# Turning C with VectorE and transfers in a fused state-space and feed-forward kernel

## The chip, the cores and the metric

The kernel runs on one core of a Trainium2 chip. The metric is the time of one execution on the device in microseconds. The core has a matrix engine (TensorE), a vector engine (VectorE), a scalar engine (ScalarE), a general engine (GpSimd, called POOL in the profile), and a synchronising engine (SyncE, SP) that here only issues transfers. All transfers run on the core's 16 DMA engines, whichever engine issues them. Results of TensorE go to PSUM, which has eight banks of 128 partitions by 512 f32 values; everything else lies in SBUF.

## The reference

```python
def A(x):                                   # x: (1, 2048, 448)
    Lam = Lambda_re + 1j * Lambda_im        # 448 complex modes
    dt = exp(log_dt)
    Lam_bar = exp(dt * Lam)
    B_bar = ((Lam_bar - 1) / Lam)[:, None] * (B_re + 1j * B_im)
    Bu = einsum("bld,pd->blp", x, B_bar)
    h[t] = Lam_bar * h[t-1] + Bu[t]         # over 2048 tokens
    return 2 * einsum("blp,dp->bld", h, C_re + 1j * C_im).real + x * Dskip
def B(x):
    return silu(x @ w1) @ w2                # 448 -> 1792 -> 448
g = sigmoid((x * gate_w).sum(-1))
out = g * A(x) + (1 - g) * B(x)
```

All inputs and the output are bf16. The kernel takes the state's rotation apart: with `Lam_bar = r * exp(i*phi)`, the input of each chunk is turned back by cos and sin of `phi * t`, a real scan with factor r runs over the tokens, and the states are turned forward again. The factor of B_bar is put into C instead, so that the readout weights are C times a complex number per mode.

## The kernel before

**Tiles.** The 2048 tokens are four chunks of 512 (`tc`) or sixteen blocks of 128 (`tb`). The 448 real and 448 imaginary parts of the modes lie in seven slots of 128 rows: slots 0 to 2 real, 4 to 6 imaginary, slot 3 the last 64 of both. For each chunk:

- `x_transposes` turns x on TensorE through PSUM into `xT` (line 508; the first chunk line 478), ScalarE or VectorE evicts it.
- `x_products` (line 663) makes tiles F (x times a 128-column block of w1; 14 a chunk) and B (x times a slot of B; 7 a chunk), two tiles as a pair in two PSUM banks. `evict` takes F through Silu on ScalarE into `aT` (line 634), and B into `U` (`UG`): for the first chunk on VectorE (line 640), else on ScalarE (line 642). Slot 3's halves are exchanged into slot 7 by two POOL transfers.
- `lanes(tc)` is the state-space part on VectorE: products of U with the tables COS and SIN (line 704 is the helper that records them all), seven scans into the f32 buffer `Gf` (line 736), a copy of Gf to bf16 in U by POOL transfers that convert (called Gb; the last chunk by ScalarE, line 746), and four products or sums that give the states `H`. For the first chunk the part ahead of the scans is written in pieces by block `b`, 512 or 1024 values a row; for the others over the whole chunk.
- `ffn2(tb)`, called G in the order: `aT` times w2 (line 774), evicted by ScalarE with the factor 1 - g into `fe` (line 780), which a POOL transfer adds onto `Tb` (line 782). `Tb` is xnat's memory, holding x * Dskip * g from `gates` (lines 836 to 850).
- `readout(tb)`, called C in the order: H times the readout weights `CP` (line 795), seven matmuls a block; VectorE multiplies by g and adds Tb (line 798), SP stores (line 801).

**Turning C.** C's rows are the output columns, and the readout wants the modes on the partitions. C is loaded into the memory of H2 after w2's load. `readout_weights(k)` (called `cp`) turns it in 64-row pieces on TensorE through two PSUM banks (line 814); ScalarE evicts one part times sc2 into `ct` (lines 822, 825), VectorE takes the other part from PSUM times sc1, adds ct and writes `CP` (lines 827, 830).

**Buffers.** U has two buffers, H four (the third shares its memory with C's rows, the fourth first holds B's rows).

**What sets the order.** The program makes a list of operations, each with the buffers that it reads and writes, a cost and a priority. A planner (`Plan.order`, lines 104 to 201) runs it through a model with those costs. TensorE's operations keep the order in which the program wrote them; every other engine takes, among the operations that could start earliest, the one with the lowest priority number. The result is one fixed list per engine, with waits on semaphores, and each engine goes through its list in order. Loads are numbered as they are written, and SP issues them in that order; POOL has a queue of its own for its transfers. The order of TensorE's work around the change is written out on lines 867 to 883.

Of the kernel before, what the change touches and what calls it, by code (L numbers as in the profile page):

```python
# [7 lines left out]
ALU = mybir.AluOpType  # L8
# [16 lines left out]
NFILL = 2  # L25
XCOL = [0, 128, 256, 320]
# [27 lines left out]
class Plan:  # L54
# [5 lines left out]
    RATE = {"pool": 300e3, "hw": 300e3}  # L60
    LAP = {"dve": 0.08, "act": 0.09}
# [42 lines left out]
    def order(self):  # L104
# [39 lines left out]
        while len(done) < len(ops):  # L144
# [5 lines left out]
            for eng, lst in cands.items():  # L150
# [9 lines left out]
                o = min((c for c in cand if c[0] <= t0 + 1e-9), key=lambda c: (c[1].prio, c[1].i))[1]  # L160
# [116 lines left out]
def bass_gated_mix__ssm_conv_s5__dense_activation_silu__prompt_kernel(nc, A_x, A_Lambda_re, A_Lambda_im, A_B_re, A_B_im, A_C_re, A_C_im,  # L277
               A_log_dt, A_Dskip, B_x, B_w1, B_w2, gate_w, out):
    with ExitStack() as ctx:
# [9 lines left out]
        xT = sb("xT", [128, 4, S_TOK], BF16)  # L289
# [3 lines left out]
        CP = sb("CP", [128, NSLOT, D_MOD], BF16)  # L293
        aT = [sb(f"aT{k}", [128, NFB, CH], BF16) for k in range(2)]
        UG = [sb(f"UG{k}", [128, 8, CH], BF16) for k in range(2)]
# [3 lines left out]
        H2C = sb("H2C", [128, 3840], BF16)  # L299
        H = [H2C[:, 0:3584].rearrange("p (s n) -> p s n", s=NSLOT) if k == 2 else sb(f"H{k}", [128, NSLOT, CH], BF16) for k in range(4)]  # L300
        Cnat = H2C[:, :].rearrange("p (b l) -> p b l", b=4)
        cnn = [f"H2_{s}" for s in range(7)] + ["H2_3i"]
# [91 lines left out]
        def load_w1(q, k, a, b):  # L394

            cols = slice(w1cuts[k], w1cuts[k + 1])
            src = B_w1[320:448, cols] if a == 3 else B_w1[128 * a:128 * b, cols].rearrange("(b p) f -> p b f", p=128)
            load(q, w1s[:, 3, cols] if a == 3 else w1s[:, a:b, cols], src, " ".join(f"w1_{k}_{i}" for i in range(a, b)),
                 256 * (b - a) * (cols.stop - cols.start))
# [11 lines left out]
        Bnat = H[3][:, :, 0:D_MOD]  # L411
        load("sp", Bnat[:, 0:3, :], A_B_re[0:384, :].rearrange("(b p) d -> p b d", p=128), "H3_0 H3_1 H3_2", 384 * 896)
        load("sp", Bnat[0:64, 3, :], A_B_re[384:448, :], "H3_3", 64 * 896)
        load("sp", Bnat[64:128, 3, :], A_B_im[384:448, :], "H3_3i", 64 * 896)
        load("sp", Bnat[:, 4:7, :], A_B_im[0:384, :].rearrange("(b p) d -> p b d", p=128), "H3_4 H3_5 H3_6", 384 * 896)
        btn = {s: [f"BT{s}_{h}" for h in range(2)] for s in range(7)}
        load_w1("sp", len(w1cuts) - 2, 0, 3)
        load_w1("sp", len(w1cuts) - 2, 3, 4)
# [8 lines left out]
        def load_C():  # L427

            for h in range(2):
                rows = lambda a: a[224 * h:224 * h + 224, :].rearrange("(b p) l -> p b l", p=56)  # L430
                to = Cnat[64 * h:64 * h + 56]
                load("sp", to[:, :, 0:448], rows(A_C_re), f"Cn0{h} " + (" ".join(cnn) if h == 0 else ""), 224 * 896)
                load("sp", to[:, :, 576:960], rows(A_C_im[:, 0:384]), f"Cn1{h}", 224 * 768)
                load("sp", to[:, :, 448:512], rows(A_C_im[:, 384:448]), f"Cn2{h}", 224 * 300)
                load("sp", to[:, :, 512:576], rows(A_C_re[:, 384:448]), f"Cn3{h}", 224 * 300)

        load_xn(1)
        load("sp", w2s[:, :, :], B_w2.rearrange("(fb p) d -> p fb d", p=128), "w2", F_FF * 896)
        load_C()
# [28 lines left out]
        def x0_transposes(q0, part, who):  # L468
# [12 lines left out]
            for h in range(2):  # L481
                src = lambda h=h: bk(tk, h).bitcast(BF16)[:, 0:256].rearrange("p (q b n) -> p q b n", q=2, n=64)
                dst = xT[:, q0:q0 + 2, 256 * part:256 * part + 256].rearrange("p q (b h n) -> p q b h n", h=2, n=64)[:, :, :, h, :]
# [11 lines left out]
        xn_of = {tc: {q: [f"xT{tc}_{h}" for h in range(2)] for q in range(4)} for tc in range(1, NCH)}  # L495
        xn_of[0] = {q: [f"xT0_{q}{part}{h}" for part in range(2) for h in range(2)] for q in range(4)}

        def x_transposes(tc, who):
# [13 lines left out]
            for h in range(2):  # L512
                src = lambda h=h: bk(tk, h).bitcast(BF16).rearrange("p (q b n) -> p q b n", q=4, b=4)
                dst = xT[:, :, tc * CH:(tc + 1) * CH].rearrange("p q (b h n) -> p q b h n", h=2, n=64)[:, :, :, h, :]
                if who[h] == "d":
                    DVE(lambda e, src=src, dst=dst: e.tensor_copy(dst, src()), [tk], [f"xT{tc}_{h}"], 0.69, 2.2, "xTe")
                else:
                    ACT(lambda e, src=src, dst=dst: e.activation(dst, src(), AF.Copy), [tk], [f"xT{tc}_{h}"], act_cost(1024), 2.2, "xTe")

# [73 lines left out]
        def b_transposes(s0, s1, who):  # L593
# [12 lines left out]
            PE(mm, [f"H3_{s}" for s in range(s0, s1)] + ["H3_3i"] * (s0 <= 3 < s1) + ["ident"], [tk], n * 4 * 0.0285, "BT")  # L606
# [16 lines left out]
        def evict(pair, tk):  # L623

            kinds = [t[0] for t in pair]
            for k, n in ((0, 2),) if pair[0][:2] == pair[-1][:2] and len(pair) == 2 else ((0, 1), (1, 1))[:len(pair)]:
# [10 lines left out]
                U, un = UG[tc % 2], f"U{tc % 2}_"  # L637
                dst = U[:, sl, :]
                if tc == 0:
                    DVE(lambda e, src=src, dst=dst: e.tensor_copy(dst, src()), [tk], [f"{un}{m}" for m in names], 0.15 + 0.53 * n, 2.6, "U")  # L640
                else:
                    ACT(lambda e, src=src, dst=dst: e.activation(dst, src(), AF.Copy), [tk], [f"{un}{m}" for m in names], act_cost(512 * n), 5, "U")  # L642
# [4 lines left out]
        def x_products(tiles, fill={}, wait=()):  # L647
# [10 lines left out]
            def steps(k, h, a, z):  # L658
                def body(pe):
                    for n, cut in list(enumerate(part[h]))[a:z]:  # L660
                        for b, ((i, p0), tile) in enumerate(zip(cut, pairs[k])):
                            tc = tile[1]
                            r = pe.matmul(bk(toks[k], b), weights(tile, p0, p0 + 64, i), xT[p0:p0 + 64, i, tc * CH:(tc + 1) * CH],  # L663
# [42 lines left out]
        def lanes(tc):  # L706
            pr = 20 + tc
            A, an = H[tc], f"H{tc}"
            U, u = UG[tc % 2], f"U{tc % 2}_"
            Gb = U  # L710
            t = f"L{tc}"
            if tc == 0:
# [20 lines left out]
            for s in (3, 0, 4, 1, 5, 2, 6) if tc else (0, 4, 1, 5, 2, 6, 3):  # L733
# [138 lines left out]
        for f in cp(0) + G(0, 1) + cp(1, 2) + G(2, 3) + cp(3):  # L872
            f()
# [45 lines left out]
```

## Time and profile before

| | |
|---|---|
| time, median of 3 runs | 141.66 us (141.62 to 142.56) |
| the profiled execution | 141.25 us |
| its span, first to last instruction | 139.5 us |
| mean granted TensorE clock | 0.998 of full |
| TensorE busy | 135.9 us (97%) |
| VectorE busy | 122.0 us (87%) |
| ScalarE busy | 90.3 us (65%) |
| GpSimd busy | 39.2 us (28%) |
| moved by the DMA engines | 14.71 MB, 17956 packets, 2835 of them under 512 bytes |

The profile is of one execution. Its time outside the kernel, 141.25, is 1.75 us more than the span, for what lies before the first and after the last instruction. A line of the groups names the code line, the engine, the operation, and the written and read tiles. In a timeline each row gives the start, the length, and how many instructions were merged into it; a bracket at the end gives the idle time before it and what ended it. VectorE's and ScalarE's operations overlap their neighbours by some 0.07 to 0.1 us, so an operation of 0.66 us can stand 0.57 to 0.59 us from the next.

### The profile page before, as it was taken

The numbers are of one execution on the slowest core, as the hardware profiler recorded it, in microseconds if no ns is written. First come the engines' busy times: TensorE is split into PE (matmuls) and PEld (weight loads), VectorE is DVE, ScalarE is ACT, GpSimd is POOL, SyncE is SP. The second block draws the span as 40 slices with busy tenths as digits, with TensorE's granted clock in tenths as the row PEclk, the third lists the DMA queues.
The fourth block names the chain that finished last, engine by engine and source line by source line (L and its number), as shares of the span: only waits on it lengthen the run. The fifth ranks groups of instructions, "written<-read, shape, count | busy, mean of one in ns | idle before, by whom it ended". The sixth has DMA issues, their size and how long they took to land.

```text
span 139.5 us, 3000 instructions
## 1 busy us (share of the span) xinstructions
PE 135.9 (97%) x1201; PEld 67.0 (48%) x1201; DVE 122.0 (87%) x179; ACT 90.3 (65%) x157; POOL 39.2 (28%) x72
## 2 busy tenths in 40 slices
PE   7999999999999999999999999999999999999992
PEld 2445454455544544455544544444455555555561
DVE  0319999999999999999999999999999999997053
ACT  3349768999989999823694887799931268312300
POOL 7134040100248440227733001824000314022220
PEclk9999999999999999999999999999999999999999
DMA  4998999510156770104976200674202322323242
GB/s 136 337 294 243 363 320 238 177 42 0 31 79 94 129 110 1 38 15 73 157 131 155 38 5 0 95 133 79 38 4 97 66 33 36 83 83 61 40 94 71
DMA packets 17956, 14.71 MB, mean 105 GB/s; under 512 B 2835, under 2 KB 17814, under 8 KB 17942
## 3 DMA queue, kind: packets, MB, share of 16 engines
q0 software_dynamic: 6064, 5.51, 24.8%
q1 hardware_dynamic: 11318, 8.65, 20.7%
q10 hardware_dynamic: 560, 0.36, 0.8%
q8 instruction: 9, 0.15, 0.4%
q14 instruction: 5, 0.04, 0.1%
HBM read 7.17 MB, written 1.84 MB: 65 GB/s over the span
## 4 chain that ended last, share of the span: by engine, by line
PE 97%; DVE 0%; issue 0%
PE ps L663 46%; PE ps L774 31%; PE ps L795 15%; PE ps L463 2%; PE ps L508 1%; PE ps L478 1%; PE ps L814 1%; PE ps L604 1%; DVE ot L798 0%; PE ps L675 0%; PE ps L464 0%; PE ps L536 0%
## 5 line engine op out<-in xcount | busy, mean ns | idle before, releaser
L663 PE MATMUL ps<-xT,w1s 64*128 64x512 bf16 x392 | 48.5, 378 | 0.0
L774 PE MATMUL ps<-w2s,aT 128*128 128x448 bf16 x224 | 43.2, 353 | 0.0
L634 ACT ACTIVATE aT<-ps 128x1024 bf16<-128x1024 f32 (+1 forms) x30 | 28.7, 969 | 8.5 <-PE ps L663 8.4
L774 PEld LDWEIGHTS ps<-w2s,aT 128*128 128x128 bf16 x224 | 21.7, 98 | 20.4 <-ACT xnat L849 0.4
L663 PEld LDWEIGHTS ps<-xT,w1s 64*128 64x128 bf16 x392 | 19.7, 94 | 22.3 <-DVE xT L486 0.7
L663 PE MATMUL ps<-xT,BT 64*128 64x512 bf16 x196 | 25.8, 376 | 0.0
L782 POOL DMA_DIRECT2D xnat<-fe x16 | 14.1, 900 | 37.9 <-ACT fe L780 37.2
L780 ACT ACTIVATE fe<-ps,g 128x448 bf16<-128x448 f32 x16 | 10.1, 632 | 21.1 <-PE ps L774 21.0
L390 POOL DMA_DIRECT2D UG<-Gf x27 | 14.7, 549 | 20.9 <-DVE Gf L736 20.4
L736 DVE TENSOR_TENSOR_SCAN Gf<-rc,gin,H 128x512 f32<-128x512 f32 x14 | 17.2, 1268 | 0.0
L795 PE MATMUL ps<-CP,H 128*128 128x448 bf16 (+2 forms) x98 | 16.4, 326 | 0.0
L663 PEld LDWEIGHTS ps<-xT,BT 64*128 64x128 bf16 x196 | 10.8, 94 | 11.1 <-DVE Gf L562 0.2
L798 DVE SCALAR_TENSOR_TENSOR ot<-ps,g,xnat 128x448 bf16<-128x448 f32 (+2 forms) x18 | 10.8, 622 | 6.0 <-issue 4.6
L390 POOL DMA_DIRECT2D UG<-UG x8 | 4.8, 597 | 29.2 <-ACT UG L642 17.4
L704 DVE TENSOR_TENSOR H<-UG,COS 128x3584 bf16<-128x3584 bf16 (+4 forms) x10 | 12.6, 1266 | 0.0
L795 PEld LDWEIGHTS ps<-CP,H 128*128 128x128 bf16 x98 | 8.9, 98 | 7.5 <-DVE k L752 0.4
L642 ACT ACTIVATE UG<-ps 128x1024 bf16<-128x1024 f32 (+1 forms) x12 | 10.7, 923 | 1.4 <-PE ps L663 1.4
L842 ACT ACTIVATE junk<-xg 128x448 bf16<-128x448 bf16 x16 | 9.2, 574 | 2.1 <-DVE xg L704 2.0
L849 ACT ACTIVATE xnat<-xnat,g 128x448 bf16<-128x448 bf16 x16 | 9.8, 671 | 0.2
L704 DVE TENSOR_TENSOR PI<-UG,SIN 128x512 bf16<-128x512 bf16 (+2 forms) x13 | 9.1, 722 | 0.0
L704 DVE TENSOR_TENSOR PO<-UG,SIN 128x1536 bf16<-128x1536 bf16 (+1 forms) x8 | 8.7, 1087 | 0.1
L736 DVE TENSOR_TENSOR_SCAN Gf<-rc,gin,H2C 128x512 f32<-128x512 f32 x7 | 8.5, 1265 | 0.0
(102 smaller groups left out, 126.5 us busy)
## 6 DMA issues: line engine op xcount, KB each, us to landing
UG<-Gf POOLq DMA_DIRECT2D x21, 128.0 KB, 2.5
xnat<-fe POOLq DMA_DIRECT2D x16, 112.0 KB, 2.6
out_dram<-ot SPq DMA_DIRECT2D x15, 112.0 KB, 1.7
w2s<-in_B_w_dram SPq DMA_DIRECT2D x1, 1568.0 KB, 11.8
xnat<-in_A_x_dram SPq DMA_DIRECT2D x3, 448.0 KB, 6.1
w1s<-in_B_w_dram SPq DMA_DIRECT2D x1, 576.0 KB, 6.2
UG<-UG POOLq DMA_DIRECT2D x8, 64.0 KB, 2.2
H2C<-in_A_C_re_dram SPq DMA_DIRECT2D x2, 196.0 KB
```

The lines of the kernel that those rows point to most:

```text
L390: P.add(q, lambda e: e.dma_start(dst, src), list(after), name.split(), 0.6 if q == "pool" else 0.5, prio, sem(), nbytes, tag="ld " + name)
L634: ACT(lambda e, src=src, dst=dst: e.activation(dst, src(), AF.Silu), [tk, "tbl"], [f"aT{tc % 2}_{m}" for m in names], act_cost(512 * n), 2 ...
L642: ACT(lambda e, src=src, dst=dst: e.activation(dst, src(), AF.Copy), [tk], [f"{un}{m}" for m in names], act_cost(512 * n), 5, "U")
L663: r = pe.matmul(bk(toks[k], b), weights(tile, p0, p0 + 64, i), xT[p0:p0 + 64, i, tc * CH:(tc + 1) * CH], start=(h == 0 and n == 0), stop=( ...
L704: DVE(lambda e: e.tensor_tensor(o, a, b, op), r, w, dve_cost(n, 2), prio, tag)
L736: DVE(lambda e, s=s, b=b, init=init: e.tensor_tensor_scan(Gf[:, s, :], rc[:, b:b + 1].to_broadcast([128, CH]), A[:, s, :], init, ALU.mult, ...
L774: r = pe.matmul(bk(tk)[:, 0:D_MOD], aT[tc % 2][:, fb, o:o + 128], w2s[:, fb, :], start=(fb == 0), stop=(fb == NFB - 1))
L780: ACT(lambda e: e.activation(f[:, :], bk(tk)[:, 0:D_MOD], AF.Copy, scale=g1[:, tb:tb + 1]), [tk, f"g1_{tc}"], [fn], act_cost(448, 1), 7, "fe")
L782: P.add("pool", lambda e: e.dma_start(Tb[:, tb, :], f[:, :], accum_op=ALU.add), [fn, f"Tb{tb}"], [f"Tb{tb}"], 0.94, 2, sem(), 115000, tag= ...
L795: r = pe.matmul(bk(tk)[:, 0:b - a], H[tc][:, s, o:o + 128], CP[:, s, a:b], start=(s == 0), stop=(s == NSLOT - 1))
L798: DVE(lambda e, tk=tk, a=a, b=b: e.scalar_tensor_tensor(ot[tb % NOT][:, a:b], bk(tk)[:, 0:b - a], g[:, tb:tb + 1], Tb[:, tb, a:b], ALU.mul ...
L849: ACT(lambda e, tb=tb: e.activation(Tb[:, tb, :], xnat[:, tb, :], AF.Copy, scale=g[:, tb:tb + 1]), [f"xd{tc}", f"g_{tc}"], [f"Tb{tb}"], ac ...
```

## The change

C is no longer turned on TensorE. Its loads stand ahead of w2's. `readout_columns` has VectorE transpose C's four row blocks in 32x32 squares into the memory of the new third U buffer, and sixteen SP transfers then carry each 32-row group to its place in CP, in runs of 64 bytes. `readout_weights` works on CP in SBUF, in place. The transposes have a priority number ahead of the first chunk's `lanes`; gates(0) is set ahead of them, gates(1) behind lanes(0). In TensorE's order G(0) to G(3) follow each other, the turning of x for chunk 1 is one pair earlier, and C(8..11) come after G(13) instead of ahead of G(12).

The first chunk's `lanes` takes the whole-chunk form of the others. U has three buffers, H three (chunk 3 uses the first chunk's), and B's rows are loaded into the third U buffer. For blocks 8 to 11 the readout is taken from PSUM by ScalarE times g into an f32 buffer, a POOL transfer adds it onto `Tb`, and SP stores Tb. The last cut of w1 is loaded in other halves. The planner's tie tolerance for VectorE goes from 1e-9 to 1e-7. `x_blocks`, which would turn x the same way, is added but not called (`XBLK` is empty), and the layout of `xT` gets the chunk as an outer index.

```diff
+L0M = True
+XT1K = 6
+UDVE = (0, 1, 2, 3, 4, 5, 6)
+OUTA = (8, 9, 10, 11)
+PRMF = (1, 0)
+CPRIO = 15
+CPP = 20.5
+GPR = (14, 20.3, 21.5, 19)
...
-        CP = sb("CP", [128, NSLOT, D_MOD], BF16)
+        CP = sb("CP", [128, NSLOT, CH], BF16)
         aT = [sb(f"aT{k}", [128, NFB, CH], BF16) for k in range(2)]
-        UG = [sb(f"UG{k}", [128, 8, CH], BF16) for k in range(2)]
+        UG = [sb(f"UG{k}", [128, 8, CH], BF16) for k in range(3)]
         PI = sb("PI", [128, NSLOT, CH], BF16)
         PO = sb("PO", [128, NSLOT, CH], BF16)
         Gf = sb("Gf", [128, NSLOT, CH], F32)
-        H2C = sb("H2C", [128, 3840], BF16)
-        H = [H2C[:, 0:3584].rearrange("p (s n) -> p s n", s=NSLOT) if k == 2 else sb(f"H{k}", [128, NSLOT, CH], BF16) for k in range(4)]
-        Cnat = H2C[:, :].rearrange("p (b l) -> p b l", b=4)
-        cnn = [f"H2_{s}" for s in range(7)] + ["H2_3i"]
+        H = [sb(f"H{k}", [128, NSLOT, CH], BF16) for k in range(3)]
+        Cnat = H[2][:, :, :].rearrange("p s n -> p (s n)").rearrange("p (b l) -> p b l", b=4)
+        cnn = [f"H2_{s}" for s in range(7)]
...
+            elif b == 4:
+                src = bass.AP(B_w1.tensor, 128 * a * F_FF + cols.start, [[F_FF, 128], [(320 - 128 * a) * F_FF, 2], [1, n]])
...
-        Bnat = H[3][:, :, 0:D_MOD]
...
+        Bnat = UG[2][:, :, 0:D_MOD]
...
-        load_w1("sp", len(w1cuts) - 2, 0, 3)
-        load_w1("sp", len(w1cuts) - 2, 3, 4)
+        load_w1("sp", len(w1cuts) - 2, 0, 2)
+        load_w1("sp", len(w1cuts) - 2, 2, 4)
...
-            for h in range(2):
-                rows = lambda a: a[224 * h:224 * h + 224, :].rearrange("(b p) l -> p b l", p=56)
-                to = Cnat[64 * h:64 * h + 56]
-                load("sp", to[:, :, 0:448], rows(A_C_re), f"Cn0{h} " + (" ".join(cnn) if h == 0 else ""), 224 * 896)
-                load("sp", to[:, :, 576:960], rows(A_C_im[:, 0:384]), f"Cn1{h}", 224 * 768)
-                load("sp", to[:, :, 448:512], rows(A_C_im[:, 384:448]), f"Cn2{h}", 224 * 300)
-                load("sp", to[:, :, 512:576], rows(A_C_re[:, 384:448]), f"Cn3{h}", 224 * 300)
-
+            n = 0
+            for b0, b1, p in ((0, 3, 128), (3, 4, 64)):
+                rows = lambda a: a[128 * b0:128 * b0 + p * (b1 - b0), :].rearrange("(b p) l -> p b l", p=p)
+                for dst, src in (((0, 448), rows(A_C_re)), ((512, 896), rows(A_C_im[:, 0:384])), ((448, 512), rows(A_C_im[:, 384:448]))):
+                    load("sp", Cnat[0:p, b0:b1, dst[0]:dst[1]], src, f"Cn{n}" + (" " + " ".join(cnn) if n == 0 else ""),
+                         p * (b1 - b0) * max(300, 2 * (dst[1] - dst[0])), None, ["Cnz"] * b0)
+                    n += 1
+
+        POOL(lambda e: e.memset(Cnat[:, 3, :], 0.0), [], ["Cnz"], 0.9, 5)
         load_xn(1)
+        load_C()
         load("sp", w2s[:, :, :], B_w2.rearrange("(fb p) d -> p fb d", p=128), "w2", F_FF * 896)
-        load_C()
         load_xn(2)
...
-                U, un = UG[tc % 2], f"U{tc % 2}_"
+                U, un = UG[tc % 3], f"U{tc % 3}_"
                 dst = U[:, sl, :]
-                if tc == 0:
-                    DVE(lambda e, src=src, dst=dst: e.tensor_copy(dst, src()), [tk], [f"{un}{m}" for m in names], 0.15 + 0.53 * n, 2.6, "U")
+                after = [f"{un}{m}" for m in names] + [un + "3i"] * (3 in names)
+                if tc == 0 and a in UDVE:
+                    DVE(lambda e, src=src, dst=dst: e.tensor_copy(dst, src()), [tk], after, 0.15 + 0.53 * n, 2.6, "U")
                 else:
-                    ACT(lambda e, src=src, dst=dst: e.activation(dst, src(), AF.Copy), [tk], [f"{un}{m}" for m in names], act_cost(512 * n), 5, "U")
+                    ACT(lambda e, src=src, dst=dst: e.activation(dst, src(), AF.Copy), [tk], after, act_cost(512 * n), 5, "U")
...
-            A, an = H[tc], f"H{tc}"
-            U, u = UG[tc % 2], f"U{tc % 2}_"
+            A, an = H[tc % 3], f"H{tc % 3}"
+            U, u = UG[tc % 3], f"U{tc % 3}_"
             Gb = U
             t = f"L{tc}"
-            if tc == 0:
+            if tc == 0 and not L0M:
...
+                if tb in OUTA:
+                    f, fn = ct[tb // 2 % 2][:, tb % 2, :], f"ct{tb // 2 % 2}{'ab'[tb % 2]}"
+                    ACT(lambda e, tk=tk, f=f: e.activation(f, bk(tk)[:, 0:D_MOD], AF.Copy, scale=g[:, tb:tb + 1]),
+                        [tk, f"g_{tc}"], [fn], act_cost(448, 1), 3, "out")
+                    P.add("pool", lambda e, f=f: e.dma_start(Tb[:, tb, :], f, accum_op=ALU.add), [fn, f"Tb{tb}"], [f"Tb{tb}"], 0.94, 2, sem(), 230000, tag="Tb+")
+                    P.add("sp", lambda e: e.dma_start(out2[t0:t0 + 128, :], Tb[:, tb, :]), [f"Tb{tb}"], [], 0.3, 1, outs[NOT], 128 * 896, tag="st")
+                    continue
...
+        ctn = [f"CT{g}{m}" for g in range(4) for m in range(4)]
+
+        def readout_columns():
+
+            C32 = UG[2][:, 0:NSLOT, :].rearrange("p s n -> p (s n)").rearrange("p (m t b i) -> p m t b i", m=4, b=4, i=32)
+            names = [f"X32_{k}" for k in range(4)]
+            held = [f"U2_{s}" for s in range(7)] + ["U2_3i"]
+            turned = [f"BT{s}_{h}" for s in range(7) for h in range(2)]
+            for b in range(4):
+                src = Cnat[:, b, :].rearrange("p (t m i) -> p t m i", m=4, i=32)
+                dst = C32.rearrange("p m t b i -> p b t m i")[:, b, :, :, :]
+                DVE(lambda e, dst=dst, src=src: e.transpose(dst, src), [f"Cn{n}" for n in range(6)] + ["Cnz"] + [CBEH] * (CBEH != "") + cnn + turned, [names[b]],
+                    0.15 + 896 / 960, CPRIO, "CTd")
+            k = sem()
+            for g in range(4):
+                for m in range(4):
+                    to = CP[32 * m:32 * m + 32, :, :].rearrange("p t (b g i) -> p (t b) g i", b=4, i=32)[:, :, g, :]
+                    P.add("sp", lambda e, to=to, g=g, m=m: e.dma_start(to, C32[32 * g:32 * g + 32, m, :, :, :].rearrange("p t b i -> p (t b) i")),
+                          names + held, [f"CT{g}{m}"], 0.66, 400, k, 57344, tag="CTm")
...
         def readout_weights(k):
 
-            tk = Ps(2)
-
-            def mm(pe):
-                for j, c0 in ((0, 128 * k), (1, 448 if k == 3 else 576 + 128 * k)):
-                    for b in range(4):
-                        o = j * 224 + 56 * b
-                        for h in range(2):
-                            p = slice(64 * h, 64 * h + 56)
-                            r = pe.transpose(bk(tk, h).bitcast(BF16)[:, o:o + 56], Cnat[p, b, c0:c0 + 128], ident[p, p])
-                return r
-            PE(mm, [f"Cn{n}{h}" for n in range(4) for h in range(2)] + cnn + ["ident"], [tk], 8 * 0.0285, "CT")
-            both_banks = lambda j: bk2(tk).rearrange("p h n -> p (h n)").bitcast(BF16).rearrange("p (h n) -> p h n", h=2)[:, :, 224 * j:224 * j + 224]
-            re = lambda: both_banks(0)
-            im = lambda: both_banks(1)
-            in_two = lambda a: a.rearrange("p (h n) -> p h n", h=2)
+            re, im = CP[:, k, 0:D_MOD], CP[:, 4 + k, 0:D_MOD] if k < 3 else None
             c, cn = ct[k % 2], f"ct{k % 2}"
-            ACT(lambda e: e.activation(in_two(c[:, 0, :]), im(), AF.Copy, scale=sc2[:, k:k + 1]), [tk, "sc2"], [cn + "a"], act_cost(448, 1), 3, "ct")
             both = [cn + "a"]
             if k < 3:
-                ACT(lambda e: e.activation(in_two(c[:, 1, :]), re(), AF.Copy, scale=sc2[:, k:k + 1]), [tk, "sc2"], [cn + "b"], act_cost(448, 1), 3, "ct")
+                ACT(lambda e: e.activation(c[:, 0, :], im, AF.Copy, scale=sc2[:, k:k + 1]), ctn + ["sc2"], [cn + "a"], act_cost(448, 1), 3, "ct")
+                ACT(lambda e: e.activation(c[:, 1, :], re, AF.Copy, scale=sc2[:, k:k + 1]), ctn + ["sc2"], [cn + "b"], act_cost(448, 1), 3, "ct")
                 both.append(cn + "b")
-            DVE(lambda e: e.scalar_tensor_tensor(in_two(CP[:, k, :]), re(), sc1[:, k:k + 1], in_two(c[:, 0, :]), ALU.mult, ALU.add),
-                [tk, "sc1"] + both, [f"CP{k}"], 0.68, 1, "CP")
+            else:
+                for a, b in ((slice(0, 64), slice(64, 128)), (slice(64, 128), slice(0, 64))):
+                    ACT(lambda e, a=a, b=b: e.activation(c[a, 0, :], CP[b, 3, 0:D_MOD], AF.Copy, scale=sc2[b, 3:4]), ctn + ["sc2"], [cn + "a"], act_cost(448, 1), 3, "ct")
+            DVE(lambda e: e.scalar_tensor_tensor(re, re, sc1[:, k:k + 1], c[:, 0, :], ALU.mult, ALU.add),
+                ctn + ["sc1"] + both, [f"CP{k}"], 0.68, CPP, "CP")
             if k < 3:
-                DVE(lambda e: e.scalar_tensor_tensor(in_two(CP[:, 4 + k, :]), im(), nsc1[:, k:k + 1], in_two(c[:, 1, :]), ALU.mult, ALU.add),
-                    [tk, "sc1"] + both, [f"CP{4 + k}"], 0.68, 1, "CP")
+                DVE(lambda e: e.scalar_tensor_tensor(im, im, nsc1[:, k:k + 1], c[:, 1, :], ALU.mult, ALU.add),
+                    ctn + ["sc1"] + both, [f"CP{4 + k}"], 0.68, CPP, "CP")
...
-                   {(1, 0): [parameters], (K - 2, 0): turn_b[:1], K - 2: turn_b[1:2], K - 1: turn_b[2:], 7: xt(1, "da") + [lambda: lanes(0)]}, [K - 2])
+                   {PRMF: [parameters], (K - 2, 0): turn_b[:1], K - 2: turn_b[1:2], K - 1: turn_b[2:], XT1K: xt(1, XT1), 8: [lambda: lanes(0)] + [readout_columns] + [lambda tc=tc: x_blocks(tc) for tc in XBLK]}, [K - 2])
         gates(0)
         gates(1)
         lanes(1)
-        for f in cp(0) + G(0, 1) + cp(1, 2) + G(2, 3) + cp(3):
+        for f in G(0, 1, 2, 3):
             f()
-        x_products(F(1) + F(2, 0, 1) + B(2), {2: xt(2, "aa")})
+        for f in cp(0, 1, 2, 3):
+            f()
+        x_products(F(1) + F(2, 0, 1) + B(2), {2: xt(2, "aa")} if 2 not in XBLK else {})
         gates(2)
         lanes(2)
         for f in G(4, 5, 6, 7) + C(0, 1, 2, 3):
             f()
-        x_products(F(2, 1) + B(3) + F(3), {1: xt(3, "aa"), 9: [lambda: gates(3), lambda: lanes(3)]})
-        for f in C(4, 5, 6, 7) + G(8, 9, 10, 11):
-            f()
-        for f in C(8, 9, 10, 11) + G(12, 13, 14, 15) + C(12, 13, 14, 15):
+        x_products(F(2, 1) + B(3) + F(3), {1: xt(3, "aa") if 3 not in XBLK else [], 9: [lambda: gates(3), lambda: lanes(3)]})
+        for f in C(4, 5, 6, 7) + G(8, 9, 10, 11, 12, 13) + C(8, 9, 10, 11) + G(14, 15) + C(12, 13, 14, 15):
```

## The prediction

> **What bounds the kernel now.** I read the page's first part and the chain that ended last, then that chain in order of time, then the timeline of VectorE at its two ends, then busy times by window. The chain's summary on the page:
>
> ```profile
> PE 97%; DVE 0%; issue 0%
> ```
>
> The reader is to see that no wait stands in it: from 0.72 us to 136.75 us each TensorE piece begins where the last one ended. In order of time, with start and length, the stretch that the change touches and the end:
>
> ```profile
> 19.64 0.47 PE ps L508 x32
> 20.10 8.20 PE ps L663 x76
> 28.31 0.21 PE ps L814 x16
> 28.51 5.40 PE ps L774 x28
> 33.92 0.52 PE ps L814 x32
> 34.44 5.40 PE ps L774 x28
> 39.84 0.31 PE ps L814 x16
> ...
> 120.79 10.59 PE ps L774 x56
> 131.38 5.35 PE ps L795 x42
> ```
>
> L814 is the turning of C: three pieces in the chain. But VectorE is nearly as full; from 10.9 us to 128.2 us it has no idle time worth naming. Its timeline at the end, with what it waited for in brackets:
>
> ```profile
> 118.54 0.66 DVE L798 SCALAR_TENSOR_TENSOR ot<-ps,g,xnat 128x448 bf16<-128x448 f32 x1
> ...
> 126.07 2.09 DVE L704 TENSOR_TENSOR H<-H,PO 128x2048 bf16<-128x2048 bf16 x2
> 132.80 0.69 DVE L798 SCALAR_TENSOR_TENSOR ot<-ps,g,xnat 128x448 bf16<-128x448 f32 x1 [4.64 <-issue]
> ```
>
> The last states (H of chunk 3) are done at 126.07 + 2.09 = 128.16 us; TensorE reads them first at 131.38 us. VectorE's slack is 3.22 us. So the time is TensorE's sum, and VectorE's sum lies 3.2 us below it. By windows (columns: stretch, TensorE, weight loads, VectorE, ScalarE, GpSimd, clock, DMA share, GB/s):
>
> ```profile
> 28.00:40.00 12.00, 12.00 (x126) 6.30 (x124) 12.00 (x26) 11.41 (x26) 2.60 (x4) 1.00 0.17 32
> 40.00:58.00 18.00, 18.00 (x203) 8.31 (x196) 17.91 (x22) 17.79 (x32) 7.07 (x12) 1.00 0.51 81
> 58.00:75.00 17.00, 17.00 (x99) 8.56 (x99) 16.97 (x16) 8.61 (x20) 7.91 (x12) 1.00 0.55 92
> ```
>
> ScalarE too is full to 58 us and half free after it; the DMA engines are nearly free from 28 to 40 us.
>
> **What TensorE loses.** The three L814 pieces: 0.21 + 0.52 + 0.31 = 1.04 us. The two ffn2 pieces among them take 5.40 us for 28 matmuls, where 56 without such neighbours take 10.59, 5.295 for 28: up to 0.21 more. Gain 1.04 to 1.25; I take 1.2, most of both. The turning of x for chunk 1 goes one pair (14 matmuls, 1.51 us) forward, to about 18.1 us; its load, issued at 9.59, takes 6.1 us by the DMA rows and is there by about 16. Moving C(8..11) behind G(12,13) reorders equal work, 0; H2 is done at 106.2, long before.
>
> **What VectorE gets and loses, up to H3.**
> - Four block transposes of 128x896, bf16. No row shows one. Below: the copy COS of 128x1536 bf16 runs 0.53 us, 0.35 ns an element, 0.31 us each. Above: the f32 scan of 128x512, 1.27 us, 2.48 ns an element, 2.2 us each. I take the plain one-input pass between them, the cast L640 of 128x1024 in 1.22 us: 1.19 ns an element, 1.06 us, 1.0 us start to start. Four: +4.0 (1.2 to 8.9).
> - The first chunk's products in whole-chunk form. Before, 27.51 to 35.20 less two CP operations (1.18 us), and 0.34 for the last sum: 6.85. After: two of 3584 (1.94 each, start to start), one of 2048 (1.14), one of 1536 (0.87): 5.89. -0.96.
> - The seven CP products read SBUF in place of PSUM; 0.59 start to start now. Down to 0.34 (the 128x512 product in SBUF) the gain would be 1.75; I take 0.
> - Four readouts less, 0.59 each (119.11 - 118.54 is 0.57): -2.4.
> Sum 4.0 - 0.96 - 2.4 = +0.64: H3 at 128.8. It is due at 131.38 - 1.2 = 130.2. **VectorE still has 1.4 us**, so all this is hidden, and what goes over 1.4 is paid in full.
>
> The Trainium skill ("VectorE: DVE Perf Modes", The three transpose paths) gives VectorE's transpose of 128x128 bf16 311 ns. As an estimate by columns, 7 x 311 = 2.2 us for one of these, as long as the scan's bound; by it the sum would be 143.9, the far end of the first rival.
>
> **C's transfers.** C's loads go ahead of w2's on SP's queue. w2 is issued at 10.07 and takes 11.8 us, so landed near 22. In the trace's single packets the last x load ends near 27.5, and its last 1024 packets (41 ns median, 16 engines) are 2.6 us of that; with C ahead and x behind, w2 ends near 24.9. It is needed at 28.3: 3.4 us of cover. C itself then lands near 17.5, before VectorE has time for it. VectorE's free place opens after 24.2 (where gates(0) stood), and four transposes end near 30.5.
>
> Sixteen transfers on SP follow, each 32 partitions x 28 runs of 64 bytes: 14336 packets. SP's issues of large loads take 0.43 to 0.51 us, the code counts 0.66: 8 to 10.6 us. The packets: in the trace's packet records on SP's queue a 128-byte packet takes 13 ns, a 4-byte one 9, a 512-byte one 27; so 11 ns for 64 bytes: 14336 x 11 / 16 = 9.9 us, as long as the issues. Done near 30.5 + 10.6 + 1.7 (the landing of an output row) = 42.8, mostly in the window with a DMA share of 0.17. Behind the sixteen on SP stand only the stores, the first at 70.3, and nobody waits for those. The clearing of C's pad on POOL (0.9 by the code's cost) falls into POOL's idle time from 4.35 to 9.3, and the other cut of w1's last load moves the same bytes: 0 for both. All 64-byte runs stay inside SBUF, which no SP transfer of this trace does; the upper bound is the POOL queue's, which does: 98 ns for 1024 bytes against 46 on SP's queue, 22 against 9 for 4 bytes, a factor of 2.1 to 2.4. But stores from SBUF on SP's queue take 41 ns for 896 bytes like loads, so I take it that the factor goes with the queue: 9.9 us.
>
> The Trainium skill ("DMA: Bandwidth & Descriptors", Specifications) says that below 512 bytes a transfer is read, changed and written back. 128 bytes in 13 ns against 512 in 27 show no such step here; by that rule alone the second rival would hold, with 142 us and more.
>
> **ScalarE.** Eight evictions of C parts (0.52 start to start, 4.2 us) move from 28 to 41 us to about 43 to 48, and gates(1) comes later too, behind the scans. Both add some 4 to 5 us to a stretch that is full. Silu and these go ahead by priority; gates(1) can wait until 58 to 75, with 8.4 us free. Behind it wait only fe of G(4), whose bank is one of eight. Cost 0, up to 1 if TensorE misses banks. Four readouts on ScalarE (0.63 each) fall after 118 us, where it is a third busy; their f32 adds on POOL (0.9 each, 2.6 to land) and one store each end near 131, ahead of the end. The third U buffer takes a reuse away that in before cost no visible wait: 0; chunk 2's U now waits for C's transfers, done 10 us earlier.
>
> **Sum.** 141.25 (profiled execution) - 1.2 = 140.05; the median shown, 141.66, is 0.41 above it, so the forecast on that scale is **140.5 us**. A measurement here can tell about 1% (1.4 us) from no change, so this counts as the same.
>
> **Rivals.**
> 1. VectorE becomes the bound. Its place is H3 before C(12); it decides from 1.4 us more than my sum, a transpose above 1.35 us, or waits of that length for Gb copies that C's transfers hold up. At 2.2 us a transpose it adds 4.8, H3 at 133.6, 3.4 late: 143.9. For it: full VectorE, no such row. Against: one-input passes lie near 1 us. 141 to 144.
> 2. Slower: C's transfers take twice as long. At 11 x 2.2 = 24 ns a packet, 14336 x 24 / 16 = 21.5 us, with the Gb copies (DMA share 0.51 from 40 to 58) done at 54 to 58 in place of 43. ScalarE's queue is in order: its C parts stand at about 43 to 48, and the silus of F(1) behind them. TensorE's eight banks hold four pairs, 4 to 6 us, then it stops: 11 to 15 less 5 is 6 to 10 us, 146.5 to 150; a transfer slower by half gives 142 to 145. It decides from about 47 us for the last landing. For it: POOL's factor. Against: the packets on SP's queue.
> 3. The exchange of loads doesn't give an earlier C for nothing: w2 lands after 28.3 and G(0) waits. A stall of SP's queue like the one of 5.37 us at 10.62 would do it, 24.9 + 5.4 = 30.3, 2 us late: 142.5. Against: the queue is full while it stalls.
>
> **Chances.** Forecast 0.55 (own range 139.8 to 141.2; 0.11 of it beyond 1% faster); rival 1 0.18 (0.06 of it over 1% slower), rival 2 0.19 (all slower), rival 3 0.08 (0.03 slower). Faster 0.11, same 0.61, slower 0.28. The range 139.8 to 144.2 leaves out 0.04 below and 0.14 of rival 2.
>
> **What would show it.** Right: no L814 in the chain and no other wait; transposes of about 1.06 us; the last of C's transfers landed by 44; the last H near 128.8 with idle VectorE behind it. Wrong: ScalarE or VectorE waiting for a transfer into CP between 43 and 58 with TensorE gaps behind; or C(12) waiting for H.

## The result and the profile after

The changed kernel takes **150.3 us** (median of 6 runs, 149.88 to 151.01), beside 141.63 us for the kernel before in the same comparison (141.56 to 142.56). The ratio is 1.060, interval 1.057 to 1.064: slower by 6%, where 140.5 us was forecast. Each ratio here and below compares fast runs; a few executions of a kernel ran in a slower state, and these count only in the ranges and medians. The profiled execution took 150.11 us with a span of 148.3, against 141.25 and 139.5.

The summary of the chain that ended last, on the page of the changed kernel, answers the 97% of before:

```profile
PE 66%; DVE 12%; SPq 8%; DMA 7%; issue 2%; ACT 1%; ACTq 1%; DVEq 0%
```

A third of the chain is no longer TensorE's. In order of time (start, length, what; the 55 longest pieces), from the last of C's transfers on:

```profile
42.82 1.33 SPq L870
44.20 6.55 DMA CP<-UG
50.77 0.67 ACT ct L879
51.44 0.92 ACT aT L675
52.41 13.68 PE ps L705 x104
66.09 10.70 PE ps L816 x56
...
140.22 5.34 PE ps L837 x42
```

Read it upwards from the fifth line. TensorE starts a piece of 104 matmuls at 52.41. It had waited for a silu (`aT`, L675), the silu for the first part of C (`ct`, L879) ahead of it on ScalarE, and that part for a transfer into `CP` which was issued from 42.82 on and landed at 50.77. Ahead of these lines the chain goes back through all of SP's issues at L870 to the transposes at L864. From 52.41 to the end it is TensorE alone, back to back, as before.

ScalarE's timeline, with its waits in brackets:

```profile
41.98 1.02 ACT L675 ACTIVATE aT<-ps 128x1024 bf16<-128x1024 f32 x1 [1.07 <-PE ps L705]
50.77 0.67 ACT L879 ACTIVATE ct<-CP,scc 128x448 f32<-128x448 bf16 x1 [7.77 <-DMA CP<-UG]
51.34 1.01 ACT L675 ACTIVATE aT<-ps 128x1024 bf16<-128x1024 f32 x1
```

ScalarE stands for 7.77 us in front of one operation of 0.67 us. The silu behind it needs nothing from C. TensorE's timeline beside it:

```profile
44.79 0.63 PE L530 MATMUL ps<-ident,xnat 64*128 64x64 bf16 x32
52.41 7.20 PE L705 MATMUL ps<-xT,w1s 64*128 64x512 bf16 x43 [6.98 <-ACT aT L675]
```

It works on for 2.4 us after ScalarE has stopped (43.0 to 45.4), then waits 6.98 us for a PSUM bank. And there is a second loss behind the wait. By windows (stretch and length; busy time and instructions of TensorE, weight loads, VectorE, ScalarE, GpSimd; granted clock, DMA share, GB/s):

```profile
48.00:50.00 2.00, 0.00 (x0) 0.00 (x0) 1.29 (x6) 0.00 (x0) 1.57 (x3) 1.00 1.05 139
50.00:52.00 2.00, 0.00 (x0) 0.00 (x0) 0.69 (x1) 1.23 (x2) 0.00 (x0) 0.56 1.16 172
52.00:54.00 2.00, 1.59 (x8) 0.59 (x10) 2.00 (x4) 2.00 (x4) 0.00 (x0) 0.50 0.30 40
...
56.00:58.00 2.00, 2.00 (x17) 0.76 (x14) 2.00 (x3) 0.72 (x2) 0.00 (x0) 0.73 0.00 0
58.00:60.00 2.00, 2.00 (x22) 0.91 (x20) 1.55 (x2) 2.00 (x3) 0.00 (x0) 1.00 0.00 0
```

The granted clock falls to half while TensorE stands idle and is full again only after 57 us. The 104 matmuls behind the gap take 13.68 us. The chain of the kernel before has the same piece without a gap:

```profile
40.15 5.40 PE ps L663 x50
45.55 0.47 PE ps L508 x32
46.02 11.22 PE ps L663 x104
```

It took 11.22 us there, so the half clock costs 2.46.

The sum of the difference in span, 148.3 - 139.5 = 8.8: gap 6.98, half clock 2.46, a later start of TensorE's work 0.44 (the small matmul at L577 begins at 9.20, its counterpart L536 of before at 8.76), less the 1.04 that TensorE saves on C (from that small matmul to the end of x's turning at L530 or L508 it takes 36.22 us, 37.26 before). That makes 8.84. The later start isn't put down to the change: in the experiments below the small matmul begins anywhere from 8.73 to 9.30 us, at 9.22 in the fourth and 8.73 in the fifth, which both load C as before.

Why was the transfer late? The DMA issues between 28 and 55 us (first the changed kernel, then the kernel before; in each row the number of issues, KB of each, median us from issue to landing):

```profile
CP<-UG SPq DMA_DIRECT2D x16, 56.0 KB, 3.5
UG<-Gf POOLq DMA_DIRECT2D x7, 128.0 KB, 4.9
```

```profile
UG<-Gf POOLq DMA_DIRECT2D x7, 128.0 KB, 2.3
```

The second row is the copies of the scans (Gb) on POOL's queue. They take twice as long beside C's transfers. From 42 to 50 us the DMA engines have a busy share of 1.08 in the windows. In the single packets of the trace, C's have 3.0 us of each engine's time in these 8 us, and POOL's queue (Gb copies, adds of `fe`) has 5.6.

### The profile page after: what moved, and what is told of

Read it like the earlier page. It is cut to its first block, busy times and chain, and to the rows that moved or that the text cites. A ratio compares the mean times of both kernels' runs of the same rounds, so it can differ in the third digit from the quotient of the medians.

```text
span 148.3 us, 2874 instructions
## 1 busy us (share of the span) xinstructions
PE 137.4 (93%) x1137; PEld 66.8 (45%) x1137; DVE 123.1 (83%) x165; ACT 93.0 (63%) x162; POOL 42.8 (29%) x77
## 4 chain that ended last, share of the span: by engine, by line
PE 66%; DVE 12%; SPq 8%; DMA 7%; issue 2%; ACT 1%; ACTq 1%; DVEq 0%
PE ps L705 30%; PE ps L816 21%; PE ps L837 14%; SPq L870 8%; DMA CP<-UG 4%; DMA w1s<-in_B_w_dram 3%; DVE UG L682 3%; DVE UG L864 2%; DVE Gf L568 2%; DVE Gf L596 1%; DVE BT L653 1%; ACTq L404 1%; DVE Gf L565 1%; DVE xg L746 1%; ACT aT L675 1%
## 5 line engine op out<-in xcount | busy, mean ns | idle before, releaser
L705 PE MATMUL ps<-xT,w1s 64*128 64x512 bf16 x392 | 50.7, 393 | 7.3 <-ACT aT L675 7.0
L675 ACT ACTIVATE aT<-ps 128x1024 bf16<-128x1024 f32 (+1 forms) x30 | 28.9, 971 | 15.1 <-PE ps L705 15.0
L705 PEld LDWEIGHTS ps<-xT,w1s 64*128 64x128 bf16 x392 | 20.4, 97 | 31.7 <-ACT aT L675 7.1
L778 DVE TENSOR_TENSOR_SCAN Gf<-rc,gin,H 128x512 f32<-128x512 f32 x21 | 25.5, 1268 | 0.1
L837 PE MATMUL ps<-CP,H 128*128 128x448 bf16 (+2 forms) x126 | 21.9, 332 | 0.0
L746 DVE TENSOR_TENSOR H<-UG,COS 128x3584 bf16<-128x3584 bf16 (+2 forms) x9 | 16.2, 1811 | 0.0
L837 PEld LDWEIGHTS ps<-CP,H 128*128 128x128 bf16 x126 | 11.6, 98 | 10.0 <-DVE Gf L778 0.4
L847 DVE SCALAR_TENSOR_TENSOR ot<-ps,g,xnat 128x448 bf16<-128x448 f32 (+2 forms) x14 | 8.2, 609 | 4.4 <-issue 3.0
L684 ACT ACTIVATE UG<-ps 128x1024 bf16<-128x1024 f32 (+1 forms) x12 | 10.6, 927 | 0.0
L746 DVE TENSOR_TENSOR PI<-UG,SIN 128x1536 bf16<-128x1536 bf16 (+1 forms) x8 | 8.6, 1086 | 0.0
L885 DVE SCALAR_TENSOR_TENSOR CP<-CP,sc1s,ct 128x448 bf16<-128x448 bf16 x4 | 2.7, 683 | 6.9 <-ACT ct L880 6.9
```

What stands on the lines that cost most here:

```text
L746: DVE(lambda e: e.tensor_tensor(o, a, b, op), r, w, dve_cost(n, 2), prio, tag)
L778: DVE(lambda e, s=s, b=b, init=init: e.tensor_tensor_scan(Gf[:, s, :], rc[:, b:b + 1].to_broadcast([128, CH]), A[:, s, :], init, ALU.mult, ...
L837: r = pe.matmul(bk(tk)[:, 0:b - a], H[tc % 3][:, s, o:o + 128], CP[:, s, a:b], start=(s == 0), stop=(s == NSLOT - 1))
```

## The experiments

The theory after the result: C's transfers land late because 14336 packets of 64 bytes share the DMA engines with POOL's queue; the time is lost because the planner, which was told 57344 bytes a transfer, put the first C part ahead of the silus on ScalarE. Rivals: the issues on SP alone make them late; the lateness is harmless and the order alone costs the time; or another part of the change (whole-chunk lanes, f32 readouts, third U buffer, order of G and C) brings the loss.

**1. The planner told a longer transfer.** Only the place of the C parts in ScalarE's list changes; the transfers are the same.

```diff
-                          names + held, [f"CT{g}{m}"], 0.66, 400, k, 57344, tag="CTm")
+                          names + held, [f"CT{g}{m}"], 0.66, 400, k, 350000, tag="CTm")
```

> The kernel after, with one number changed: the planner is told that each of C's sixteen transfers moves 350000 bytes in place of 57344, so that it believes the last one landed near 51 us, and puts ScalarE's first C part behind more of F(1)'s silus. No work, no transfer and no wait is taken away. Theory (ScalarE's in-order queue stood at a C part from 43.0 to 50.8 us with F(1)'s silus behind it): the last landing stays at 50 to 51 us, the TensorE gap of 7.0 us and the half clock behind it (2.5 us) go, 150.3 - 9.5 = 140.8 us, 140.2 to 142.0. Rival (C's transfers or VectorE's transposes themselves hold TensorE up, wherever the C parts stand): 147 us or more, with TensorE gaps left between 43 and 60 us.

Measured 142.66 us (142.07 to 143.56) beside 141.77 of before, ratio 1.008 (1.005 to 1.012), span 140.3. The first C part now stands at 52.56 on ScalarE, TensorE runs through from 45 to 54 us at full clock, and 7.6 us of the loss are gone. So the order on ScalarE makes the stall out of a late transfer. But it isn't as fast as before, and the timelines of ScalarE and TensorE show where:

```profile
77.94 0.58 ACT L900 ACTIVATE junk<-xg 128x448 bf16<-128x448 bf16 x1 [1.65 <-DVE xg L746]
...
79.58 2.65 PE L705 MATMUL ps<-xT,w1s 64*128 64x512 bf16 x20 [0.87 <-ACT aT L675]
```

VectorE, delayed by 1.57 us in front of Gb copies (5.0 us to land), brings `gates(2)` late, ScalarE waits for it with silus behind, and TensorE loses 0.87 us at 78.7. It takes 23.25 us for this piece of 202 matmuls where the kernel before takes 21.90, so 1.35 are lost there in all. With the 1.04 saved and a start 0.54 later that gives the 0.8 by which the span exceeds 139.5. It is the same pattern at another place.

**2. The same bytes in long rows.** 512 packets of 1792 bytes instead of 14336 of 64. C's squares then don't come to their places in CP, so this kernel leaves the right readout out, and only its time counts.

```diff
-                    to = CP[32 * m:32 * m + 32, :, :].rearrange("p t (b g i) -> p (t b) g i", b=4, i=32)[:, :, g, :]
-                    P.add("sp", lambda e, to=to, g=g, m=m: e.dma_start(to, C32[32 * g:32 * g + 32, m, :, :, :].rearrange("p t b i -> p (t b) i")),
+                    to = CP[32 * m:32 * m + 32, :, :].rearrange("p t n -> p (t n)")[:, 896 * g:896 * g + 896]
+                    P.add("sp", lambda e, to=to, g=g, m=m: e.dma_start(to, C32[32 * g:32 * g + 32, m, :, :, :].rearrange("p t b i -> p (t b i)")),
```

> The kernel after, with C's sixteen transfers writing whole rows of 1792 bytes in place of 28 runs of 64 (same bytes, same number of transfers, 512 packets in place of 14336; C's squares land in other places, so the readout is of another C). Theory A (the number of packets makes the transfers late): the last lands near 31.1 + 16 x 0.7 + 2 = 44 us, ScalarE waits 1 to 2 us, no TensorE gap, 140.8 to 142 us. Theory B (the sixteen transfers as such, or the SBUF-to-SBUF way, are slow beside the POOL transfers): the last landing stays at 49 us or later and the time at 149 to 150.5 us.

A single run: 140.62 us, span 138.8. SP's issues and ScalarE's first C part:

```profile
30.91 10.15 SPq L870 DMA_DIRECT2D CP<-UG  x16
```

```profile
43.29 0.67 ACT L879 ACTIVATE ct<-CP,scc 128x448 f32<-128x448 bf16 x1 [0.52 <-DMA CP<-UG]
```

With few packets the issues run through in 10.15 us instead of 14.68, the transfers land in 2.1 us instead of 3.5, and the C part that ScalarE reaches first waits 0.52 us. The list of orders is that of the changed kernel. The chain is TensorE from 6.06 us on. So the small packets cause the lateness, not SP's issuing as such, and about 140.6 is what the change gives when C comes in time (experiment 8 finds the same in twelve runs).

**3. The Gb copies of chunk 0 taken off POOL's queue.** ScalarE converts them instead, as the last chunk's; C's transfers are unchanged.

```diff
-                    if tc + 1 < NCH:
+                    if 0 < tc and tc + 1 < NCH:
```

> The kernel after, with the first chunk's nine Gb copies made by ScalarE in place of POOL transfers, so that from 42 us on nothing but C's transfers and two adds of fe is on the DMA engines. Theory A (C's 64-byte packets get the smaller share of the engines while Gb runs): the last of C's transfers lands at 44.5 to 47 us in place of 50.8; time 142 to 146 us with ScalarE busier by 5 us. Theory B (64-byte packets need that long by themselves): the last landing stays at 49.5 us or later.

A single run: 145.62 us, span 143.8. ScalarE's wait and TensorE's gap:

```profile
46.18 0.67 ACT L879 ACTIVATE ct<-CP,scc 128x448 f32<-128x448 bf16 x1 [3.06 <-DMA CP<-UG]
```

```profile
47.81 6.39 PE L705 MATMUL ps<-xT,w1s 64*128 64x512 bf16 x42 [2.79 <-ACT aT L675]
```

C lands at 46.18 instead of 50.77, 4.6 us earlier. The issues start 0.4 earlier here (30.73 against 31.14), so the Gb copies account for some 4.2 us of the delay. The remaining 3.4 us over the forecast 42.8 can be followed in this run: the transposes end 0.2 later than reckoned (30.7), undisturbed issues stand 0.70 us apart where 0.66 was taken (16 x 0.04 = 0.6), and the last transfer takes 2.3 us to land, the shortest in the trace, where 1.7 was taken (0.6). Alone they would be there at 30.7 + 16 x 0.70 + 2.3 = 44.2. What is left, 2.0, fits the stretches from 36 to 39 and 41 to 44 us, where the adds of `fe` run on POOL's queue and issues are up to 1.5 us apart; no run took those adds away, so that share is argued.

**4. Two other parts alone, on the kernel before:** whole-chunk lanes for chunk 0 and the four f32 readouts, with C turned by TensorE as before.

```diff
-            if tc == 0:
+            if False:
...
+                if tb in (8, 9, 10, 11):
+                    ACT(lambda e, tk=tk, f=f: e.activation(f, bk(tk)[:, 0:D_MOD], AF.Copy, scale=g[:, tb:tb + 1]),
+                        [tk, f"g_{tc}"], [fn], act_cost(448, 1), 3, "out")
+                    P.add("pool", lambda e, f=f: e.dma_start(Tb[:, tb, :], f, accum_op=ALU.add), [fn, f"Tb{tb}"], [f"Tb{tb}"], 0.94, 2, sem(), 230000, tag="Tb+")
+                    P.add("sp", lambda e: e.dma_start(out2[t0:t0 + 128, :], Tb[:, tb, :]), [f"Tb{tb}"], [], 0.3, 1, outs[NOT], 128 * 896, tag="st")
+                    continue
```

> The kernel before, with two parts of the change and nothing of C's turning: the first chunk's lanes in whole-chunk form and the four f32 readouts. Theory (they only take VectorE time off, about 1.0 + 2.4 us, and VectorE has slack at the end): last H earlier by 2 to 3.5 us, time 141.4 to 141.9 us, the same as before. Rival (one of the two holds TensorE up or delays the end, and is a share of the loss): 143 us or more.

Measured 141.92 us (141.41 to 142.35), ratio 1.001 (0.998 to 1.004): no difference. VectorE's last H ends at 124.30 + 2.09 = 126.39 us, 1.8 earlier than before, a little less than expected; nobody waits for it.

**5. C's turning put back on TensorE in the changed kernel.** The other side of the same question: its loads, matmuls, evictions and place in the order are those of before, all else is the change.

```diff
-CPP = 20.5
+CPP = 1
...
-            re, im = CP[:, k, 0:D_MOD], CP[:, 4 + k, 0:D_MOD] if k < 3 else None
+            tk = Ps(2)
+
+            def mm(pe):
...
+                            r = pe.transpose(bk(tk, h).bitcast(BF16)[:, o:o + 56], Cnat[p, b, c0:c0 + 128], ident[p, p])
...
         load_xn(1)
+        load("sp", w2s[:, :, :], B_w2.rearrange("(fb p) d -> p fb d", p=128), "w2", F_FF * 896)
         load_C()
-        load("sp", w2s[:, :, :], B_w2.rearrange("(fb p) d -> p fb d", p=128), "w2", F_FF * 896)
```

> The kernel after with C's turning put back: C turned by TensorE, loaded behind w2, evicted from PSUM as before. Kept are the three U buffers, the first chunk's lanes in whole-chunk form, the order of TensorE's work at the end, the gates' order and the four f32 readouts. Theory (the whole loss came with C's transfers): 141.2 to 142.0 us, the same as before, all of the chain on TensorE. Rival (another part carries a share of the loss): 143 us or more.

Measured 141.7 us (141.22 to 142.8), ratio 1.000 (0.997 to 1.003). The whole loss is gone, and so is the whole gain: without C's new way the rest of the change does nothing to the time that can be measured here. VectorE isn't the bound, it idles 6.81 us ahead of its last outputs:

```profile
132.77 0.68 DVE L847 SCALAR_TENSOR_TENSOR ot<-ps,g,xnat 128x448 bf16<-128x448 f32 x1 [6.81 <-issue]
```

**6. C earlier.** The transposes go ahead of the rest of the first chunk's phase tables, of gates(0) and of the last of its U evictions, so that C's transfers are past before the Gb copies start, and the planner is told 250000 bytes.

```diff
-CPRIO = 15
+CPRIO = 2.9
...
-                          names + held, [f"CT{g}{m}"], 0.66, 400, k, 57344, tag="CTm")
+                          names + held, [f"CT{g}{m}"], 0.66, 400, k, 250000, tag="CTm")
```

> The kernel after, with two numbers changed: VectorE's four transposes of C get priority 2.9 in place of 15, ahead of the phase tables and gates(0), so that C's transfers start near 25 us in place of 31; and the planner is told 250000 bytes a transfer, so that it puts the first C part at about 40 us. Theory (the transfers came late because they started at 31 us and lost the engines to fe and Gb from 36 us on): the last lands at 38 to 41 us, no wait of ScalarE over 1 us, no TensorE gap, Gb copies land in 2.5 to 3 us again; 140.3 to 141.2 us, below before by 0.3 to 1%. Rival (w2 or the x loads lose the engines to 14336 small packets from 25 us on, and G(0) waits for w2): TensorE gap near 28.5 us, 142 us or more.

Measured 141.25 us (140.68 to 143.43) beside 141.81, ratio 0.998 (0.994 to 1.001). SP issues from 25.16 to 37.72, the transfers land in 2.4 us, no C part waits for one, and the Gb copies take 3.1. What keeps it from the 140.6 of the second experiment is, as far as the trace shows, a crowd on ScalarE between 41 and 46 us. Four C parts stand among the silus there, three of them ahead of the first (41.34, 41.90, 42.46, and 43.93), and TensorE waits at 45.3:

```profile
45.55 4.92 PE L705 MATMUL ps<-xT,w1s 64*128 64x512 bf16 x43 [0.29 <-ACT aT L675]
```

**7. The same with all readouts on VectorE.**

```diff
-OUTA = (8, 9, 10, 11)
+OUTA = ()
```

> As the run with the early transposes, but the four readouts of blocks 8 to 11 go back to VectorE (2.4 us more for it before the last H). By the prediction's sum VectorE has 1.4 us of slack at the last H with them on ScalarE, so without: last H 1.0 us late, 141.3 to 142.2 us, with a TensorE gap of about 1 us ahead of C(12). Rival (VectorE's slack is larger than its sum says): same time as the run with the early transposes, no gap.

A single run: 143.33 us, span 141.4, above the 142.2 that was expected at most. The last line of VectorE's work on H, in the sixth experiment's timeline and in this one's:

```profile
127.41 2.08 DVE L746 TENSOR_TENSOR H<-H,PO 128x2048 bf16<-128x2048 bf16 x2
```

```profile
131.00 2.09 DVE L746 TENSOR_TENSOR H<-H,PO 128x2048 bf16<-128x2048 bf16 x2
```

H is complete 3.6 us later, at 133.09, and TensorE's last readouts start at 133.14 instead of 131.09. Of the 3.6, the four readouts are 2.4 (4 x 0.59), the waits of VectorE for a Gb copy 1.0 (1.2 against 0.2 us). VectorE had 1.6 us to spare, so 2.0 reach the end, where about 1.0 was expected. Here VectorE is the bound, which is the first rival of the prediction, and the four f32 readouts are what keeps it from being so in the changed kernel.

**8. C early, its parts late.** The two causes apart: transfers ahead of the Gb burst, and the C parts behind the silus.

```diff
-CPRIO = 15
+CPRIO = 2.9
...
-                          names + held, [f"CT{g}{m}"], 0.66, 400, k, 57344, tag="CTm")
+                          names + held, [f"CT{g}{m}"], 0.66, 400, k, 380000, tag="CTm")
```

> As the run with the early transposes, but the planner is told 380000 bytes a transfer, so that ScalarE's C parts stand behind the first silus of F(1), some 8 us behind the real landing. Theory (what is left there over TensorE's own sum is a gap of about 0.4 us near 45 us, where C parts stand ahead of silus): that gap goes, all of the chain from 6 us on is TensorE, the span is 138.5 to 139.0 and the time 0.5 to 1.0% below before. Rival (C parts that stand late crowd ScalarE between 49 and 60 us, or C(0) waits for CP): 141.3 us or more, no better than the run with the early transposes.

Measured **140.66 us** (140.24 to 142.51, 12 runs) beside 141.81 (17 runs), ratio 0.994 (0.991 to 0.997). This is below both kernels; beside the kernel before it is only 0.6%, but the interval lies clear of 1. The chain in order of time over the stretch that was lost, and at the end:

```profile
39.46 5.50 PE ps L705 x50
44.96 0.47 PE ps L530 x32
45.43 11.22 PE ps L705 x104
56.65 10.70 PE ps L816 x56
...
130.79 5.34 PE ps L837 x42
136.16 0.35 DVE ot L847
```

No wait and no half clock: the 104 matmuls take 11.22 again. Its span, 138.9, is the 139.5 of before less the 1.04 saved, plus a start 0.45 later (L577 at 9.21). VectorE's last H ends at 128.31 + 2.08 = 130.39, 0.4 us ahead of the readouts that need it. In this order more than 0.4 us can't be taken from TensorE without taking it from VectorE too.

## Why the prediction was wrong

**The step that failed** is the one on C's transfers: "Done near 30.5 + 10.6 + 1.7 (the landing of an output row) = 42.8, mostly in the window with a DMA share of 0.17." They were done at 50.77. The price of a packet was not the fault. 64 bytes inside SBUF took 8 ns in the median and 9.7 in the mean where 11 were taken, so all of them are 14336 x 9.7 / 16 = 8.7 us of the engines' time (9.9 reckoned). The fault was to sum them as if they had the engines to themselves. The forecast end, 42.8, lies already in the next window of the table shown, with a share of 0.51, and the sum gave the neighbours on POOL's queue nothing. Experiment 3 prices the Gb copies at 4.2 us, experiment 2 shows that few packets would have gone through in time.

**The loss went the way of the second rival.** It named the wait, ScalarE's order with the silus behind, TensorE's hold-out in the PSUM banks, and 47 us as the landing from which it decides; its 146.5 to 150 us lie just under the 150.3 measured. Its price came from another mechanism (POOL's factor of 2.2 per packet, which SP's queue doesn't show) and led to a landing of 54 to 58. With the landing that was measured, its own sum (50.8 - 43, less 5) gives 2.8 us and some 143, so that its range came near is luck. The banks held TensorE for 2.4 us after ScalarE stopped, less than the 4 to 6 given there. So the landing that hurts lies earlier than 47: in experiment 3, at 46.18, the gap was already 2.79. And neither it nor the forecast had the half clock behind the gap, 2.46 us.

**ScalarE**: "Cost 0, up to 1 if TensorE misses banks" was an argument about load. The loss came from order: one operation whose input was late held up all that stood behind it on ScalarE. With the input in time the cost is small or nothing (the 104 matmuls take 0.2 longer in experiment 2, the same in experiment 8), and with C early but its parts among the silus (experiment 6) it is the 0.3 us of a missed bank.

**What held.** The transposes were taken at 1.06 us each. VectorE's timeline:

```profile
27.94 1.10 DVE L864 STREAM_TRANSPOSE UG<-H 128x896 bf16<-128x896 bf16 x1
...
29.02 2.09 DVE L864 STREAM_TRANSPOSE UG<-H 128x896 bf16<-128x896 bf16 x2
...
136.51 2.09 DVE L746 TENSOR_TENSOR H<-H,PO 128x2048 bf16<-128x2048 bf16 x2
```

1.05 to 1.10 each. The estimate of 2.2 us, worked out by columns from the figure of the Trainium skill ("VectorE: DVE Perf Modes", The three transpose paths), was twice too high. VectorE's last H at 138.60 contains 8.9 us of new waits (6.9 for C's parts, 2.0 for a Gb copy); without them it would be 129.7 by this estimate, and in experiments 2 and 6, where C comes in time, it is 129.5; 128.8 was reckoned. The slack of 1.4 us was of the right size: it is 1.6 in experiment 6 and 0.4 in experiment 8, and experiment 7 shows that what goes beyond it is paid. The CP products gained nothing from reading SBUF (0.68 us, 0.60 apart), as taken. w2, issued at 15.40 behind C, landed 9.8 us later at 25.2 (24.9 reckoned, 28.3 needed), so the third rival didn't come. TensorE's gain, taken at 1.2, is 1.04: the three pieces at L814, and nothing of the 0.21 hoped for beside them (the 56 matmuls of G take 10.70 us, not 10.59, and the 50 behind them 5.50, not 5.40). The forecast of 140.5 is what experiments 2 and 8 measure: 140.6 and 140.7. The forecast was that of a kernel in which C isn't waited for.

## What to carry to other kernels

Add up a new transfer together with the transfers of the other queues in the stretch where it will run to its end, not with the share that the stretch had where it starts. Where its consumer stands in an engine's ordered list ahead of work on the critical path, the delay of the transfer is the delay of everything behind it, so a late or uncertain input belongs behind that work (here 7.6 us, for one number in a planner's cost). And a gap in TensorE's work costs more than its length when the clock drops in it.

## What was unexpected of the hardware

**The granted clock.** In finer windows of the changed kernel the matmuls stop at 45.4, the clock drops to 0.50 near 50.2 (4.8 us later), and it is full again near 57.1 (4.7 us after the restart at 52.41). In experiment 3 a gap of 2.79 us was enough: the matmuls stop at 45.0, and the clock drops to 0.50 at 48.3 and stays there until some 51.7, although they had begun again at 47.81. The row by windows:

```profile
48.00:50.00 2.00, 2.00 (x14) 0.76 (x12) 1.91 (x8) 2.00 (x3) 0.00 (x0) 0.58 0.00 0
```

Gaps of 0.87 us (experiment 1) and 0.29 (experiment 6) left it at 1.00, and the matmuls went on at their full pace of 22 in 2 us. The Trainium skill ("TensorE: Matmul & The Clock Gate", Part 1) says that half rate comes after an idle window of about 3.4 us and full rate after about 3.4 us of sustained work, in windows that run freely. The first gap agrees with that; the second, shorter than a window, was not to be expected by it. What does agree is the length of the half rate: about 6.8 us (50.2 to 57.1) in the one case and 3.4 (48.3 to 51.7) in the other, two and one of these windows. In the 3.4 us ahead of the second drop TensorE had still worked for some 0.6 (to 45.0, and again from 47.81), so here a window counted as idle without being empty; how much work would have kept the clock no run shows.

**Sharing between queues.** From 42 to 50 us 4467 packets of C's and 950 of POOL's queue went through, 4.7 for each one, in 3.0 and 5.6 us of the engines' time. From 39 to 40 us, with POOL's queue almost still, 1522 of C's went in one microsecond; from 46 to 47, beside 170 of POOL's at about 97 ns each, 209. The Trainium skill ("DMA: Bandwidth & Descriptors", Queues, rings and completion order) says that an engine takes turns between the queues, draining a group of some 9 to 17 descriptors from one before it turns to the next. The trace agrees in that a queue of small pieces loses time to one of large pieces; the length of a turn isn't to be read from it. No step is seen for pieces below 512 bytes: 64 bytes took 8 ns, 128 took 13 and 512 took 27.
